# Block-diagonal projection weights and four smaller moves in a fused linear-attention and gated-MLP kernel

## The chip, the cores and the metric

The kernel runs on one core of a Trainium2 chip. The metric is device time in microseconds (us) of one execution; the median of the runs counts. The engines are TensorE (PE; its weight loads are PEld), VectorE (DVE), ScalarE (ACT), GpSimd (POOL) and SyncE (SP), which issues most DMAs.

## The reference

```python
# q, k, v: (8, 8, 576, 64); omega: (128, 64); w_gate, w_val: (512, 1536); w_out: (1536, 512)
scale = 64 ** -0.25
def phi(x):
    proj = np.einsum('bhsd,md->bhsm', x, omega)
    h = proj - np.sum(x * x, axis=-1, keepdims=True) / 2.0
    h = h - np.max(h, axis=-1, keepdims=True)
    return np.exp(h) / np.sqrt(128)
q_p, k_p = phi(q * scale), phi(k * scale)
kv = np.einsum('bhsm,bhsd->bhmd', k_p, v)
z = np.sum(k_p, axis=2)
num = np.einsum('bhsm,bhmd->bhsd', q_p, kv)
den = np.einsum('bhsm,bhm->bhs', q_p, z)[..., None] + 1e-06
x = (num / den).transpose(0, 2, 1, 3).reshape(4608, 512)
g = x @ w_gate
out = (g * (1 / (1 + np.exp(-g))) * (x @ w_val)) @ w_out      # all float32
```

## The kernel before

The attention goes in 72 steps of two groups. A group is 256 rows of two heads of q or of k (or, once per batch element, the 64 rows left over of all eight heads). The first 6 steps have two groups of k, the next 60 one of q and one of k, the last 6 two of q. Stages of several steps are in flight at once:

- `st_transpose(n)`: four TensorE transposes (`pt`) turn the rows of step n, so that the two heads of a group lie one above the other, 64 rows each; ScalarE copies them to `x`, GpSimd squares the rows (`sq`).
- `st_project(n)` (L434): `x` times `omT`, which holds the scaled omega twice, in rows 0 to 63 and in 64 to 127. For each of two groups and two chunks of 128 rows, one matmul per head, on that head's 64 rows. Head 0 writes PSUM bank `pp[0]`, head 1 bank `pp[1]`. An fp32 matmul becomes two instructions, so 8 matmuls stand as 16 in the trace; a transpose stands as one.
- `st_max`, `st_exp`: VectorE's sums and maxima (L448, L455), and eight exponentials on ScalarE into `ph`.
- `k_accumulate(n)`, two steps later: `ph` of k times v, with a column of ones for z, summed in bank `kvacc`; after the last group of a batch element and four heads `kv_finalize` copies it to `kvr`.
- For q of batch elements 0 to 3: `q_transpose` (`ptq`, copied to `qt`), `q_mult` (`po`), a division on VectorE, and `q_out` (`xt`, turned by TensorE, split into `xh` and `xl`).
- For q of elements 4 to 7 the division comes first: `kv_finalize` turns z on TensorE (`zp`) and sends it by DRAM back to all partitions (`zd`, then `zt` in `load_z`); `q_den` multiplies `ph` by z on GpSimd (`jk`) and sums on VectorE; `q_norm` scales `ph` on GpSimd (L548); then `q_transpose` and `q_out` (L653, `kvr` as the stationary operand, one head to each half of the columns).

The MLP follows as rows of x are complete. Three tiles of 512 rows come in visits (L689: gate and value; L698: the output product), the other six in pairs (L928) after the attention. Each fp32 operand is split in a high and a low part and multiplied in three fp32r products. The weights are converted for that by `convert_all` in 36 pieces of 128 x 512, six ticks each, on ScalarE, VectorE and GpSimd, and stored in DRAM (`wscr`).

The order of the work is written out: `CLOSE` lists the stages of a step below `EARLY` (25), `GROUPED` those from there on, with places (`SHARE`) into which the MLP's matmuls are dealt by a course computed in advance. `marks` says how many pieces are to be converted by which step (`want` is `OPS`, 6 ticks, times the mark): from step 6 on, 4.5 by step 25, 9 by step 28. Inside that order each engine's program is laid out by a scheduler, so neighbours can swap.

PSUM has eight banks of 128 x 512 fp32: three for the MLP (`ps_m`, also used by early steps), two for `pp` (`ps_p`), one with tag "b" (`ps_att`), one with tag "t" (`ps_tr`), one for `kvacc` (`ps_k`). `pt` lies in "t". From step 25 on `xt` of a step's first q lies in "t", of a second q in "b"; `ptq` of a first q in "b", of a second in "t".

Of the kernel before, what the change touches and what calls it, by code (L numbers as in the profile page):

```python
# [11 lines left out]
F32 = mybir.dt.float32  # L12
# [11 lines left out]
def kernel(  # L24
# [11 lines left out]
    nc = tc.nc  # L36
# [61 lines left out]
    def ps_att(name, shape):  # L98
        return ps_a.tile(shape, F32, name=name, tag="b")
# [106 lines left out]

    EARLY = whole[1]
    clock = course + 4.0 * np.arange(NN + 1)
    marks = [(6, 0.0), (EARLY, 1.5 * FA), (EARLY + 3, 3 * FA)]
    FIRST_RAW = marks[0][0] - 2  # L210
    for k_ in range(1, NSET):
        at = int(np.searchsorted(course, cum[len(ROUNDS[0]) * k_ - 1]))
# [124 lines left out]

    omT = const.tile([P, M], F32, name="omT")  # L340

    def setup_omega():
        om2 = accp.tile([P, 2, D], F32, name="om2", tag="acc")
        for j in range(2):
            nc.scalar.dma_start(om2[:, j, :], omega)
        pt = ps_moe("pt_om", [P, M])
        nc.tensor.transpose(pt, om2.rearrange("p a d -> p (a d)"), ident)
        nc.scalar.activation(omT, pt, AF.Copy, scale=SCALE)

# [71 lines left out]
    def st_project(n):  # L423
        if n >= NS:
            return
        x, st, sq = sts[n]

        new = ps_moe if n < EARLY and n % 2 else ps_proj
        pp = [new(f"pp{hh}_{n}", [P, 2, CH, M]) for hh in range(2)]
        for i in range(2):  # L430
            for c in range(CH):
                for hh in range(2):
                    r = slice(hh * D, (hh + 1) * D)
                    nc.tensor.matmul(  # L434
                        pp[hh][:, i, c, :], x[r, i, c * P : (c + 1) * P], omT[r], start=True, stop=True
                    )
        sts[n] = st, sq, pp
        return True

# [2 lines left out]
    def st_max(n):  # L442
        if n >= NS:
            return
        st, sq, pp = sts[n]

        with tc.issue_after(biased[0].ins) if biased else ExitStack():
            nc.vector.tensor_reduce(  # L448
                st[:, 0].rearrange("p i c h -> p (i c h)"),
                sq.rearrange("p i c h d -> p (i c h) d"),  # L450
                axis=AX.X,
                op=ALU.add,
            )
        for hh in range(2):
            nc.vector.tensor_reduce(st[:, 1, :, :, hh], pp[hh], axis=AX.X, op=ALU.max, negate=True)  # L455
        s0, s1, s2, s3 = (st[:, j].rearrange("p i c h -> p (i c h)") for j in range(4))
        nc.vector.scalar_tensor_tensor(s2, s0, SQC, s1, op0=ALU.mult, op1=ALU.add)
        biased[:] = [nc.vector.scalar_tensor_tensor(s3, s0, -SQC, s2, op0=ALU.mult, op1=ALU.add)]  # L458
        step_end["v"] = biased[0]
        return True  # L460

    def st_exp(n):
        if n >= NS:
            return
        st, _, pp = sts.pop(n)
        for i, (kind, b, g) in enumerate(steps[n]):
            ph = att.tile([P, CH, 2 * M], F32, name=f"ph{i}_{n}", tag=f"ph{i}", bufs=3)
            for hh in range(2):
                for c in range(CH):
                    step_end["s"] = nc.scalar.activation(  # L470
                        ph[:, c, hh * M : (hh + 1) * M], pp[hh][:, i, c, :],
                        AF.Exp, bias=st[:, 3, i, c, hh : hh + 1], scale=1.0,
                    )
            box[kind, b, g] = ph
        return True
# [7 lines left out]
    def kv_finalize(b, a2):  # L483
        acc = kvacc.pop((b, a2))
        raw = att.tile([P, 4, VW], F32, name=f"kvr{b}_{a2}", tag="kvr", bufs=4)
        nc.scalar.copy(raw, acc)
        for j in range(2):
            kvst[b, 2 * a2 + j] = raw[:, 2 * j : 2 * j + 2, :]
        if b >= BPOOL:

            zp = ps_att(f"zp{b}_{a2}", [4, P])
            nc.tensor.transpose(zp, raw[:, :, D], ident)
            zs = att.tile([4, P], F32, name=f"zs{b}_{a2}", tag="zs")
            nc.scalar.copy(zs, zp)
            zd = dram.tile([4, P], F32, name=f"zd{b}_{a2}", tag="zd", bufs=4)
            nc.sync.dma_start(zd, zs)
            zds[b, a2] = zd

    zds = {}
    zbc = {}  # L500

    def load_z(n):

        for _, b, g, gr in slots(n, "q"):
            if g == 0 and b >= BPOOL:
                zt = att.tile([P, 2, 4, M], F32, name=f"zt{b}", tag="zt")
                for a2 in range(2):
                    nc.sync.dma_start(
                        zt[:, a2], zds.pop((b, a2)).rearrange("(o h) m -> o h m", o=1).broadcast_to([P, 4, M])
                    )  # L510
                    zbc[b, a2] = zt[:, a2]
# [28 lines left out]

    def q_norm(n):
        n -= NLAG
        for _, b, g, gr in slots(n, "q"):
            if b < BPOOL:
                continue
            dn = dns.pop((b, g))
            phv = box["q", b, g].rearrange("p c (h m) -> p (c h) m", m=M)
            nc.gpsimd.tensor_tensor(  # L548
                phv, phv,
                dn[:, 2].rearrange("p c (h o) -> p (c h) o", o=1).broadcast_to([P, 2 * CH, M]),  # L550
                op=ALU.mult,
            )
# [31 lines left out]
    qts = {}  # L584
    xns = {}

    def q_transpose(n):
        m = n
        todo = [(b, g) for _, b, g, gr in slots(n - TLAG, "q") if b < BPOOL]
        todo += [(b, g) for _, b, g, gr in slots(n - NLAG, "q") if b >= BPOOL]  # L590
        for i, (b, g) in enumerate(todo):
            ph = box.pop(("q", b, g))
            pt = (ps_moe if m < EARLY else ps_tr if i else ps_att)(f"ptq{b}_{g}", [P, 2, G])
            for hh in range(2):
                for c in range(CH):
                    nc.tensor.transpose(pt[:, hh, c * P : (c + 1) * P], ph[:, c, hh * M : (hh + 1) * M], ident)  # L596
            qts[b, g] = att.tile([P, 2, G], F32, name=f"qt{b}_{g}", tag="qt", bufs=4)
            nc.scalar.copy(qts[b, g], pt)
# [39 lines left out]
    def q_out(n):  # L638
        n -= OLAG
        for i, b, g, gr in slots(n, "q"):  # L640
            po = (ps_att if n + OLAG < EARLY or i else ps_tr)(f"xt{b}_{g}", [P, G])
            first = column(b, gr)
            if b < BPOOL:
                xn = xns.pop((b, g))
                for c in range(CH):
                    nc.tensor.transpose(po[:, c * P : (c + 1) * P], xn[:, c].rearrange("p h d -> p (h d)"), ident)  # L646
            else:
                qt = qts.pop((b, g))

                segs = [(pr, pr * RES, RES) for pr in range(NPAIR)] if gr is None else [(gr[0], 0, G)]  # L650
                for pr, o, w in segs:
                    for hh in range(2):
                        nc.tensor.matmul(  # L653
                            po[hh * D : (hh + 1) * D, o : o + w], kvst[b, pr][:, hh, 0:D], qt[:, hh, o : o + w],
                            start=True, stop=True, skip_group_check=True,
                        )
            j, o = tile_of(first)
            if gr is None:
                parts_ = [(po.rearrange("d (r c) -> d r c", c=RES), slice(0, NPAIR), j, o, RES)]
            else:  # L660
                cut = min(TILES[j][1] - o, G)
                parts_ = [(po[:, 0:cut], gr[0], j, o, cut)]
                if cut < G:
                    parts_.append((po[:, cut:G], gr[0], j + 1, 0, G - cut))
            for src, pr, j, o, w in parts_:
                if j in x_dram:
                    xo = att.tile(list(src.shape), F32, name=f"xo{b}_{g}_{j}", tag="xo", bufs=3)
                    nc.scalar.copy(xo, src)
                    nc.sync.dma_start(x_dram[j][:, pr, o : o + w], xo)
                    continue  # L670
                if j not in xt:
                    xt[j] = [xres.tile([P, NPAIR, T], F32R, name=f"x{e}{j}", tag=f"x{e}") for e in "hl"]
                hi, lo = (t[:, pr, o : o + w] for t in xt[j])
                nc.scalar.copy(hi, src)
                nc.vector.tensor_tensor(lo, src, hi.bitcast(F32), op=ALU.subtract)
            if gr is None or gr[0] == NPAIR - 1:
                cols_done[0] = first + (RES if gr is None else G)
        return bool(slots(n, "q"))
# [388 lines left out]
    def give(us):  # L1067
# [28 lines left out]
        q_den,  # L1096
    )
    GROUPED = (
        q_out,
        st_project,  # L1100
        q_transpose,
# [84 lines left out]
```

## Time and profile before

| | us |
|---|---|
| runs | 1176.55, 1169.88, 1171.24 |
| median | 1171.24 |
| profiled execution | 1174.65 |
| its span, first to last instruction | 1172.6 |
| TensorE busy | 1145.0 |
| VectorE / ScalarE / GpSimd busy | 703.3 / 684.7 / 588.6 |
| pp, busy time of its 1152 matmuls (L434) | 96.0 |
| normalisation on GpSimd (L548), 36 | 38.2 |

A row of the timeline gives start, length, engine, line, operation, output and inputs, the stationary and moving shapes, the count, and in brackets the idle time of the engine before it and what ended it. A row of the waits gives who waited for whom, us in total, times, and the longest.

### The profile page before, as it was taken

How to read it: one execution, taken by the hardware profiler on the slowest of the kernel's cores; microseconds unless marked ns; L12 is line 12 of the kernel's file. 1: busy time of each engine (PE TensorE's matmuls, PEld its weight loads, DVE VectorE, ACT ScalarE, POOL GpSimd, SP SyncE). 2: the span in 40 equal slices, each digit the busy share in tenths (PEclk: the TensorE clock that was granted, in tenths of full speed). 3: DMA queues.
4: the chain of work that ended last, by engine and by line, in shares of the span. 5: the costliest groups of instructions: out<-in, count | busy, mean ns of one | idle time of the engine just before them, and what ended most of it. 6: DMA issues, size and time to landing. Idle time of an engine off the chain costs nothing.

```text
span 1172.6 us, 18833 instructions
## 1 busy us (share of the span) xinstructions
PE 1145.0 (98%) x6633; PEld 948.3 (81%) x6633; DVE 703.3 (60%) x1266; ACT 684.7 (58%) x1541; POOL 588.6 (50%) x515
## 2 busy tenths in 40 slices
PE   8999999999999999999999999999999999999998
PEld 7888778888787778767778788888878888888886
DVE  3777576454666665556373566666566666456654
ACT  4888887877766866857434544444444445444441
POOL 3332353253656775586335655544455543555551
PEclk9999999999999999999999999999999999999999
DMA  6655355654445543431445111124211111211103
GB/s 141 160 135 132 102 161 142 185 151 122 129 130 139 143 140 102 109 86 55 135 109 151 57 55 55 54 65 124 63 50 46 52 52 46 81 55 54 46 18 72
DMA packets 173965, 114.30 MB, mean 97 GB/s; under 512 B 125840, under 2 KB 144304, under 8 KB 173872
## 3 DMA queue, kind: packets, MB, share of 16 engines
q1 hardware_dynamic: 172528, 112.78, 35.1%
q8 instruction: 52, 0.85, 0.3%
q10 hardware_dynamic: 1344, 0.33, 0.1%
q14 instruction: 41, 0.34, 0.1%
HBM read 87.88 MB, written 25.18 MB: 96 GB/s over the span
## 4 chain that ended last, share of the span: by engine, by line
PE 80%; DVE 7%; ACT 4%; POOL 3%; DMA 3%; issue 2%; SPq 0%; POOLq 0%; DVEq 0%; ACTq 0%
PE o L698 22%; PE a L928 16%; PE c L928 8%; PE g L689 6%; PE pp L434 6%; PE kvacc L572 5%; PE v L689 4%; PE d L928 4%; PE pt L411 3%; PE po L613 3%; PE ptq L596 2%; ACT ph L470 2%; PE xt L653 1%; POOL wlo L252 1%; PE xt L646 1%
## 5 line engine op out<-in xcount | busy, mean ns | idle before, releaser
L470 ACT ACTIVATE ph<-pp,st 128x128 f32<-128x128 f32 x576 | 157.3, 387 | 12.8 <-DVE st L458 12.3
L728 DVE TENSOR_TENSOR acc<-o,acc 128x512 f32<-128x512 f32 x156 | 105.8, 685 | 94.6 <-PE o L698 94.2
L418 POOL TENSOR_TENSOR sq<-nat 128x512 f32<-128x512 f32 x72 | 78.1, 1084 | 156.2 <-DVE st L448 113.5
L915 POOL TENSOR_TENSOR wlo<-wspare,whi 128x512 fp32r<-128x512 f32 (+1 forms) x60 | 60.9, 1036 | 117.4 <-ACT whi L914 111.0
L455 DVE TENSOR_REDUCE st<-pp 128x4 f32<-128x512 f32 x144 | 92.8, 683 | 43.2 <-PE pp L434 42.8
L434 PE MATMUL pp<-omT,x 64*128 64x128 f32 x1152 | 96.0, 296 | 3.4 <-ACT x L419 2.3
L252 POOL TENSOR_TENSOR wlo<-wraw,whi 128x512 fp32r<-128x512 f32 x59 | 82.5, 1404 | 26.9 <-ACT whi L251 23.0
L434 PEld LDWEIGHTS pp<-omT,x 64*128 64x128 f32 x1152 | 78.2, 195 | 20.8 <-issue 10.1
L915 POOL TENSOR_TENSOR wlo<-s,whi 128x512 fp32r<-128x512 f32 x64 | 82.4, 1306 | 3.8 <-ACT whi L914 3.8
L1024 ACT COPY late<-a 128x512 f32<-128x512 f32 x72 | 42.2, 586 | 60.0 <-PE a L928 58.8
L698 PE MATMUL o<-whi,late 128*128 128x512 f32 x192 | 74.5, 389 | 0.0
L572 PE MATMUL kvacc<-v,ph 128*128 128x65 f32 x512 | 69.1, 276 | 0.0
L536 DVE TENSOR_REDUCE dj<-jk 128x4 f32<-128x512 f32 x36 | 24.6, 684 | 73.3 <-POOL jk L532 60.7
L572 PEld LDWEIGHTS kvacc<-v,ph 128*128 128x128 f32 x512 | 66.4, 200 | 0.5
L789 POOL TENSOR_TENSOR hl<-sl,hh 128x512 fp32r<-128x512 f32 x36 | 46.9, 1306 | 34.6 <-ACT hh L788 34.6
L291 POOL TENSOR_TENSOR wc<-st 128x512 int32<-128x512 int32 x36 | 37.4, 1040 | 47.7 <-ACT st L289 25.2
L419 ACT COPY x<-pt 128x512 f32<-128x512 f32 x72 | 43.2, 600 | 28.3 <-PE pt L411 26.9
L689 PE MATMUL g<-xh,whi 128*128 128x512 f32 x144 | 59.5, 414 | 0.0
L1028 DVE TENSOR_TENSOR late<-c,late 128x512 f32<-128x512 f32 x25 | 17.3, 692 | 69.7 <-PE c L928 60.6
L698 PE MATMUL o<-whi,hh 128*128 128x512 f32 x144 | 58.4, 406 | 0.5 <-ACT sl L765 0.4
L689 PE MATMUL v<-xh,whi 128*128 128x512 f32 x144 | 57.7, 401 | 0.0
L689 PE MATMUL g<-xh,wlo 128*128 128x512 f32 x144 | 57.4, 398 | 0.0
(255 smaller groups left out, 3355.7 us busy)
## 6 DMA issues: line engine op xcount, KB each, us to landing
wraw<-wscr SPq DMA_DIRECT2D x63, 256.0 KB, 2.7
wspare<-wscr SPq DMA_DIRECT2D x60, 256.0 KB, 2.7
wscr<-wc SPq DMA_DIRECT2D x36, 256.0 KB, 2.2
out_dram<-acc SPq DMA_DIRECT2D x72, 128.0 KB, 2.4
nat<-in_k_dram SPq DMA_DIRECT2D x64, 128.0 KB, 3.0
nat<-in_q_dram SPq DMA_DIRECT2D x64, 128.0 KB, 3.1
v<-in_v_dram SPq DMA_DIRECT2D x62, 128.0 KB, 3.6
st<-in_moe_w_gate_dram SPq DMA_DIRECT2D x12, 512.0 KB, 3.9
```

Source lines behind the costliest of these rows:

```text
L252: nc.gpsimd.tensor_tensor(lo, raw, hi.bitcast(F32), op=ALU.subtract)
L418: nc.gpsimd.tensor_tensor(sq, nat, nat, op=ALU.mult)
L434: nc.tensor.matmul(pp[hh][:, i, c, :], x[r, i, c * P : (c + 1) * P], omT[r], start=True, stop=True)
L455: nc.vector.tensor_reduce(st[:, 1, :, :, hh], pp[hh], axis=AX.X, op=ALU.max, negate=True)
L470: step_end["s"] = nc.scalar.activation(ph[:, c, hh * M : (hh + 1) * M], pp[hh][:, i, c, :], AF.Exp, bias=st[:, 3, i, c, hh : hh + 1], scal ...
L572: nc.tensor.matmul(acc[:, 2 * (pr % 2) + hh, :], ph[:, c, hh * M : (hh + 1) * M], vt[:, 2 * c + j if gr is None else c, hh, :], start=firs ...
L689: nc.tensor.matmul(ps, a_[:, ws], b_[:, c, :], start=n == 0, stop=n == 3 * NC - 1)
L698: nc.tensor.matmul(ps, a_[:, ts_], b_, start=first and n == 0, stop=last and n == 2)
L728: nc.vector.tensor_tensor(a_, po, a_, op=ALU.add)
L789: nc.gpsimd.tensor_tensor(hl, h, hh.bitcast(F32), op=ALU.subtract)
L915: nc.gpsimd.tensor_tensor(lo, src_, hi.bitcast(F32), op=ALU.subtract)
L928: nc.tensor.matmul(ps, a_[:, w_], b_[:, c, :], start=start and c == 0 and m == 0, stop=c == CH - 1 and m == 2, skip_group_check=True,)
```

## The change

1. `omT` becomes a block diagonal of 128 rows and 2 x 128 columns: omega for head 0 in the upper left, for head 1 in the lower right, zeros elsewhere. A projection is one matmul of 128 rows and 256 columns for each group and chunk, four in a step, and a bank `pp[i]` now holds group i with both heads. The maxima go by group.
2. The conversion of the weights begins with step 5 and has other marks: 6 by step 25, 9 by step 29.
3. `zp`, its copy and its store leave `kv_finalize` for `z_rows`, which stands first in `GROUPED`, so at the head of the next step.
4. `xt` of both q of a step lies in one tile of bank "t". From step 68 on (`KV_END`), `ptq` of a second q lies in the bank of `kvacc`, which nothing else needs by then.
5. In steps with two q, the 12 normalisations of the last six, `q_norm` runs on VectorE. (24 stay on GpSimd.)

```diff
-    marks = [(6, 0.0), (EARLY, 1.5 * FA), (EARLY + 3, 3 * FA)]
+    marks = [(5, 0.0), (EARLY, 2 * FA), (EARLY + 4, 3 * FA)]
...
-    omT = const.tile([P, M], F32, name="omT")
+    omT = const.tile([P, 2, M], F32, name="omT")
...
-        nc.scalar.activation(omT, pt, AF.Copy, scale=SCALE)
+        for j in range(2):
+            r = slice(j * D, (j + 1) * D)
+            nc.vector.memset(omT[r, 1 - j], 0.0)
+            nc.scalar.activation(omT[r, j], pt[r], AF.Copy, scale=SCALE)
...
-        pp = [new(f"pp{hh}_{n}", [P, 2, CH, M]) for hh in range(2)]
+        pp = [new(f"pp{i}_{n}", [P, CH, 2, M]) for i in range(2)]
         for i in range(2):
             for c in range(CH):
-                for hh in range(2):
-                    r = slice(hh * D, (hh + 1) * D)
-                    nc.tensor.matmul(
-                        pp[hh][:, i, c, :], x[r, i, c * P : (c + 1) * P], omT[r], start=True, stop=True
-                    )
+                nc.tensor.matmul(
+                    pp[i][:, c].rearrange("p h m -> p (h m)"),
+                    x[:, i, c * P : (c + 1) * P],
+                    omT.rearrange("p h m -> p (h m)"),
+                    start=True, stop=True,
+                )
...
-        for hh in range(2):
-            nc.vector.tensor_reduce(st[:, 1, :, :, hh], pp[hh], axis=AX.X, op=ALU.max, negate=True)
+        for i in range(2):
+            nc.vector.tensor_reduce(st[:, 1, i], pp[i], axis=AX.X, op=ALU.max, negate=True)
...
-                        ph[:, c, hh * M : (hh + 1) * M], pp[hh][:, i, c, :],
+                        ph[:, c, hh * M : (hh + 1) * M], pp[i][:, c, hh, :],
...
         if b >= BPOOL:
-
+            zraw[b, a2] = raw
...
+    def z_rows():
+
+        for (b, a2), raw in zraw.items():
             zp = ps_att(f"zp{b}_{a2}", [4, P])
...
+                if (b, 1) not in zds:
+                    z_rows()
...
+        by = nc.vector if len(slots(n, "q")) == 2 else nc.gpsimd
...
-            nc.gpsimd.tensor_tensor(
+            by.tensor_tensor(
...
+    KV_END = max(n for n in range(NS) if slots(n, "k")) + KLAG + 1
...
-            pt = (ps_moe if m < EARLY else ps_tr if i else ps_att)(f"ptq{b}_{g}", [P, 2, G])
+            if i and m >= KV_END:
+                pt = ps_k.tile([P, 2, G], F32, name=f"ptq{b}_{g}", tag="kv")
+            else:
+                pt = (ps_moe if m < EARLY else ps_tr if i else ps_att)(f"ptq{b}_{g}", [P, 2, G])
...
-            po = (ps_att if n + OLAG < EARLY or i else ps_tr)(f"xt{b}_{g}", [P, G])
+            if n + OLAG < EARLY:
+                po = ps_att(f"xt{b}_{g}", [P, G])
+            else:
+                if i == 0:
+                    both = ps_tr(f"xt{b}_{g}", [P, 2, G])
+                po = both[:, i]
...
     GROUPED = (
+        lambda n: z_rows(),
         q_out,
```

TensorE's program in an early step, 13, before (a name's last number tells buffers apart; `pp_13_911` and `pp_13_912` are the banks of head 0 and head 1, which go on in turn until each has four):

```order
L572 MATMUL kvacc_1_682<-v_103,ph_10_764 128x65 x2
L434 MATMUL pp_13_911<-omT,x_863 128x128
L613 MATMUL po_4_868<-kvr_0_369,qt_4_824 128x65 x4
L434 MATMUL pp_13_912<-omT,x_863 128x128
...
L646 MATMUL xt_4_926<-ident,xn_4_876 128x128 x2
L411 MATMUL pt_931<-ident,nat_769 128x128 x4
```

And of the changed kernel:

```order
L586 MATMUL kvacc_1_653<-v_104,ph_11_800 128x65
L632 MATMUL po_4_832<-kvr_0_352,qt_4_791 128x65 x4
L435 MATMUL pp_13_875<-omT,x_827 128x256 x2
L435 MATMUL pp_13_876<-omT,x_827 128x256 x2
L414 MATMUL pt_888<-ident,nat_731 128x128 x4
L670 MATMUL xt_4_883<-ident,xn_4_840 128x128 x2
```

The eight matmuls of 64 rows are four of 256 columns, one bank after the other, and here `po` no longer stands between two of them. (A step is split in this way in 16 of the steps 4 to 25 before, in 12 after.)

TensorE's program around step 55, where z of element 5 is turned, before (the `g` rows are the MLP's, `zp` is the turned z):

```order
L689 MATMUL g_7_5034<-xl_641,whi_0_4638 128x512
L492 MATMUL zp_0_4992<-ident,kvr_0_4990 4x128
L572 MATMUL kvacc_1_4998<-vrest_105,ph_52_4790 128x65 x4
...
L653 MATMUL xt_1_5081<-qt_1_4984,kvr_0_4037 64x256 x2
L434 MATMUL pp_55_5090<-omT,x_5029 128x128
L434 MATMUL pp_55_5091<-omT,x_5029 128x128
...
L596 MATMUL ptq_2_5100<-ident,ph_53_4902 128x128 x4
```

And of the changed kernel:

```order
L713 MATMUL g_8_4836<-xh_611,wlo_0_4442 128x512
L503 MATMUL zp_0_4858<-ident,kvr_0_4773 4x128
L677 MATMUL xt_1_4864<-qt_1_4767,kvr_0_3856 64x256 x2
L435 MATMUL pp_55_4873<-omT,x_4806 128x256 x2
L435 MATMUL pp_55_4874<-omT,x_4806 128x256 x2
L615 MATMUL ptq_2_4879<-ident,ph_53_4689 128x128 x4
```

`zp` moved from a place two matmuls into step 54's MLP work to the head of step 55, behind the whole of that work.

GpSimd's program at the first steps with two q to normalise, before (`jk` is q times z, L548 the normalisation, `hl` the MLP's):

```order
L532 TENSOR_TENSOR jk_6_6398<-ph_66_6294,zt_5723 128x512
L532 TENSOR_TENSOR jk_7_6404<-ph_66_6299,zt_5723 128x512
L548 TENSOR_TENSOR ph_66_6294<-ph_66_6294,dj_6_6400 128x512
L548 TENSOR_TENSOR ph_66_6299<-ph_66_6299,dj_7_6406 128x512
L789 TENSOR_TENSOR hl_6_6422<-sl_6_6194,hh_6_6421 128x512
L418 TENSOR_TENSOR sq_6637<-nat_6345 128x512
```

And of the changed kernel:

```order
L545 TENSOR_TENSOR jk_6_6123<-ph_66_6029,zt_5482 128x512
L545 TENSOR_TENSOR jk_7_6129<-ph_66_6034,zt_5482 128x512
L813 TENSOR_TENSOR hl_6_6147<-sl_6_5933,hh_6_6146 128x512
L421 TENSOR_TENSOR sq_6359<-nat_6080 128x512
L541 TENSOR_TENSOR jk_8_6243<-ph_67_6113,zt_5482 64x256 x4
```

The two normalisations left GpSimd; on VectorE each now stands behind the reciprocal that it needs.

More of the change, by code (lines that the diff above doesn't have):

```diff
@@ L489, in kv_finalize @@
         if b >= BPOOL:
+            zraw[b, a2] = raw
+    zraw = {}
+    zds = {}
+    def z_rows():
+        for (b, a2), raw in zraw.items():
             zp = ps_att(f"zp{b}_{a2}", [4, P])
@@ L497, in kv_finalize @@
             zds[b, a2] = zd
-    zds = {}
+        zraw.clear()
     zbc = {}
```

## The prediction

> **What bounds the kernel now.** I read the page's busy times and its chain first, then TensorE's waits, then stretches, then single steps on TensorE.
>
> ```profile
> span 1172.6 us, 18833 instructions
> ...
> PE 1145.0 (98%) x6633; PEld 948.3 (81%) x6633; DVE 703.3 (60%) x1266; ACT 684.7 (58%) x1541; POOL 588.6 (50%) x515
> ...
> PE 80%; DVE 7%; ACT 4%; POOL 3%; DMA 3%; issue 2%; SPq 0%; POOLq 0%; DVEq 0%; ACTq 0%
> ```
>
> TensorE is busy for all but 27.6 us of the span and makes 80% of the chain that ended last. Ends of matmuls are modelled, so that alone would not prove it full; the starts below do. The next question is what it ever waits for. The longest of its waits in the attention (us in total, times, longest):
>
> ```profile
> PE ptq L596 <- ACT xo L668: 3.0, 3, 2.1
> PE pt L411 <- issue: 2.3, 1, 2.3
> PE zp L492 <- ACT kvr L486: 2.1, 3, 1.1
> PE pt L411 <- ACT qt L598: 1.9, 1, 1.9
> PE pt L411 <- DVE xl L675: 1.2, 1, 1.2
> ```
>
> No engine holds TensorE up for more than a few us in all. By stretches (us; the first number of each pair is TensorE's busy time):
>
> ```profile
> core 0: us, PE busy (x) PEld busy (x) DVE busy (x) ACT busy (x) POOL busy (x), PEclk, DMA share, GB/s
> 60.00:95.00 35.00, 34.70 (x340) 31.75 (x340) 27.15 (x75) 30.18 (x91) 12.72 (x12) 1.00 0.55 139
> 130.00:160.00 30.00, 26.41 (x188) 22.06 (x187) 20.79 (x39) 25.08 (x54) 15.31 (x14) 1.00 0.48 141
> 500.00:530.00 30.00, 27.25 (x178) 20.74 (x175) 19.11 (x39) 16.27 (x44) 24.64 (x24) 0.94 0.28 75
> 530.00:560.00 30.00, 27.45 (x180) 21.09 (x179) 17.76 (x37) 21.46 (x55) 21.61 (x21) 1.00 0.22 62
> ```
>
> So a microsecond of TensorE work added in the attention (0 to 570 us) is a microsecond of time nearly everywhere, and what the change can take away is the idle of 130 to 160 and of 500 to 560 us, about 9 us.
>
> **Part 1, omega as a block diagonal.** This decides. A step's projection before is 8 fp32 matmuls, each issued as two instructions of 128 columns on 64 rows; the two heads use different halves of the array's rows. After, it is 4 matmuls, so 8 instructions of 256 columns on all 128 rows, half of them against zeros. A step of before at 164 us
>
> ```profile
> 163.64 0.38 PE L646 MATMUL xt<-ident,xn 128*128 128x128 f32 x2
> 163.95 1.16 PE L434 MATMUL pp<-omT,x 64*128 64x128 f32 x16
> 165.04 0.66 PE L596 MATMUL ptq<-ident,ph 128*128 128x128 f32 x4
> ```
>
> and at 401 us
>
> ```profile
> 400.45 0.65 PE L653 MATMUL xt<-qt,kvr 128*64 128x256 f32 x4
> 401.03 1.16 PE L434 MATMUL pp<-omT,x 64*128 64x128 f32 x16
> 402.12 0.66 PE L596 MATMUL ptq<-ident,ph 128*128 128x128 f32 x4
> ```
>
> and at 65 us
>
> ```profile
> 64.45 1.16 PE L434 MATMUL pp<-omT,x 64*128 64x128 f32 x14
> 65.54 0.44 PE L646 MATMUL xt<-ident,xn 128*128 128x128 f32 x2
> 65.81 0.60 PE L411 MATMUL pt<-ident,nat 128*128 128x128 f32 x4
> 66.25 0.56 PE L572 MATMUL kvacc<-v,ph 128*128 128x65 f32 x4
> ```
>
> with the first two of the next step ahead of po:
>
> ```profile
> 67.58 0.48 PE L434 MATMUL pp<-omT,x 64*128 64x128 f32 x2
> 67.99 1.11 PE L613 MATMUL po<-kvr,qt 128*128 128x65 f32 x8
> ```
>
> From the start of pp to the start of what follows, the 16 take 1.09 us, 68 ns each. One fp32 instruction of 128 columns, alone on the array, has a slot of (66.25 - 65.81) / 4 = 110 ns (the transposes pt). So the 16 run partly side by side, two heads at a time. The full-width form has no such partner. Its price comes from two rows:
>
> ```profile
> L653 PE MATMUL xt<-qt,kvr x192: 219/379/690, 309.4 to 570.7; 128*64 128x256 f32 x128, 128*64 128x64 f32 x64
> L434 PE MATMUL pp<-omT,x x1152: 272/272/580, 6.4 to 546.4; 64*128 64x128 f32 x192
> ```
>
> The median xt has 256 columns and lasts 379 ns, the pp with 128 lasts 272: 128 columns more cost 107 ns, so 256 columns stream in 214 ns. Bounds of a slot: below, 110 ns (the transpose's, were columns free); above, 228 ns (the 214 plus a margin of 14, an estimate). I take 214, the row of the same size, so 8 x 0.214 = 1.71 us per step.
>
> Middle: 2 transposes ahead need 0.22 of the 0.31 us before pp, so entering the 64-row form costs 0.09; before is 1.18, the change +0.53. Late: xt ahead uses half the columns, and its switch stays, so +0.62. Early: pp is mostly split around po (1.09 + 0.41 + two switches of 0.09 = 1.68), so +0.03 for a split step and +0.53 for a whole one. How many steps (16 instructions each):
>
> ```profile
> core 0: us, PE busy (x) PEld busy (x), PEclk, DMA share, GB/s
> 0.00:26.00 26.00, 8.32 (x64) 7.14 (x64) 1.00 0.65 149
> 26.00:130.00 104.00, 31.86 (x352) 24.60 (x352) 1.00 0.53 129
> 130.00:316.00 186.00, 24.33 (x320) 20.31 (x320) 1.00 0.53 148
> 316.00:560.00 244.00, 31.49 (x416) 26.13 (x416) 0.99 0.41 113
> ```
>
> Early 22 steps: in the order of before, 16 are split and 6 whole: 0.5 + 3.2 = +3.7. Middle 20 x 0.53 = +10.6. Late 26 x 0.62 = +16.1. Some five steps of before already run up to 0.5 us longer than 1.09: -2. Sum **+28 us**, none of it covered, since TensorE's queue goes straight on with the next work.
>
> The first four steps are slower by a factor of about two:
>
> ```profile
> 10.23 2.08 PE L434 MATMUL pp<-omT,x 64*128 64x128 f32 x16 [0.67 <-ACT x L419]
> 12.25 1.11 PE L411 MATMUL pt<-ident,nat 128*128 128x128 f32 x4
> 13.15 3.08 PE L572 MATMUL kvacc<-v,ph 128*128 128x65 f32 x14
> ```
>
> The four pt take 0.90 us there against 0.44 later, although the PEclk column says 1.00. At that pace 8 x 0.428 = 3.42 against 2.02: +1.4 each, +5.6 if all four stay slow. [...] Between -4 and +5.6 I take +2, a little to the side of the slow slots that the trace does show.
>
> [...]
>
> Two half-height copies of omT and two memsets at the start replace one copy: 0 to +0.3. Maxima and exponentials keep number and size; the first maximum can begin after half of the matmuls.
>
> **Part 2, z at the next step's head.** The same 8 transposes, 8 copies and DMAs. The three waits of zp on kvr (2.1 us) go, since a whole step's head lies between: -2 (0 to -2.1). Its DMAs and the broadcast issue later on SP's queue, but two steps ahead of the first q_den that reads them.
>
> **Part 3, both turned x in one bank; the second turned q in the kv bank.** Only for steps with two q, the last ones. The turned q no longer waits for xo (3.0 us), and pt no longer for qt (1.9). Now pt waits for both xo instead; the turned q stands ahead of it as cover.
>
> **Part 4, twelve normalisations from GpSimd to VectorE.** Two of them in a row, and a VectorE operation of the same size:
>
> ```profile
> 520.10 2.04 POOL L548 TENSOR_TENSOR ph<-ph,dj 128x512 f32<-128x512 f32 x2
> 520.29 0.68 DVE L785 TENSOR_TENSOR sl<-v,sl 128x512 f32<-128x512 f32 x1
> ```
>
> GpSimd gives up 12 x 1.02 = 12 us of its 46 in 500 to 560; VectorE takes 12 x 0.68 = 8 on its 37 of 60, where each now stands ahead of the next pair's small operations; a turned q waits for it as it did for GpSimd's. Parts 3 and 4 serve the same waits: 3.0 + 1.9, and 0.06 x 30 = 1.8 us for the 0.94 in the clock column: -5 (0 to -6.7).
>
> **Part 5, conversion begins at step five, 6 pieces instead of 4.5 by step 25, 9 by step 29 instead of 28.** The work is the same. The waits of pt at 136 and 159 us (1.2 + 2.3) stand behind xl, and xl behind conversion on VectorE. Fewer pieces there, and pp between xt and pt lasts 0.5 us longer: -2 (0 to -3.5). Its price is 1.5 pieces more in 26 to 130 us for ScalarE, which has three operations of this size in a piece:
>
> ```profile
> L289 ACT ACTIVATE st<-st x36: 648/726/768, 42.9 to 496.2; 128x512 int32<-128x512 uint32 x36
> ```
>
> That is 1.5 x 3 x 0.73 = 3.3 us on an engine busy 30.18 of 35: hidden as long as TensorE is the fuller one, +3 if not.
>
> **The sum.** +28 +2 -2 -5 -2 = +21, and 1 more of the 3 for ScalarE's early pieces: +22. The profiled execution took 1174.65 us (span 1172.6), 3.4 above the median 1171.24; so 1196.7 in that execution, **1193** in the median's terms.
>
> **Rivals.** [...] *Nothing given back*: the slow start costs +5.6, ScalarE becomes the bound of the early steps (+3), and of the 9 only 3 come: +34, 1205. *Faster*: the full-height instruction does not pay by column. At the transposes' 110 ns a step has 0.88 us, 0.83 less than the forecast's, 72 times: 22 - 60 = -38, 1133. It turns from slower to faster at (28 + 2 - 9 + 1) / 72 = 0.31 less per step, 1.40 us, 175 ns an instruction; the xt row says 214. *No change that can be told*: 165 to 185 ns an instruction.
>
> **Chances.** Forecast 0.58, full clock early 0.17, nothing given back 0.17, no change 0.04, faster 0.04; the last two are small because they need a slot that no row of 256 columns shows. The range 1181 to 1207 takes in the first three with 2 us beyond the ends; a measurement of this kernel tells 0.5% (5.9 us) from no change. All three are slower by more: slower 0.92, same 0.04, faster 0.04.
>
> **What would show it.** Right: pp appears 576 times with 128x256, its busy time goes from 96.0 to about 120 us, 1.71 us from its start to the next kind; TensorE's waits at zp, at ptq for xo and at pt near 522 us are gone, GpSimd's L548 group has 24. Wrong: pp's slot is under 180 ns; or the first 26 us shrink; or new waits stand before pp (on x) or ptq (on the normalisations now queued on VectorE). From 610 us on nothing should differ but the shift.

## Result: 2.5% slower, and the profile after

The changed kernel takes 1201.42 us (median of 4 runs, 1200.76 to 1204.94) against 1173.34 for the kernel before (4 runs): ratio 1.0246, 95% interval 1.0206 to 1.0286, so +28 us. The forecast was 1193 in 1181 to 1207, +22 on the median of 1171.24 that it started from. Ratios compare fast runs alone; the one slow run, of the block diagonal with x ahead, took 1958.85 us at a granted clock of 0.557 and counts only in that kernel's median.

The page after: totals, the group of pp, and the chain that ended last.

```profile
span 1199.6 us, 17638 instructions
...
PE 1174.6 (98%) x6057; PEld 975.0 (81%) x6057; DVE 718.3 (60%) x1280; ACT 685.6 (57%) x1540; POOL 579.6 (48%) x503
...
PE 85%; DVE 8%; issue 2%; DMA 2%; POOL 2%; ACT 2%; SPq 0%; POOLq 0%; DVEq 0%; ACTq 0%
...
L435 PE MATMUL pp<-omT,x 128*128 128x256 f32 x576 | 147.2, 395 | 1.8 <-ACT x L422 1.7
```

The span grew by 27.0 us, TensorE's busy time by 29.6, with 1195 instructions fewer in all and 576 fewer on TensorE. One step's projection in the middle of the attention and a late one:

```profile
163.25 0.38 PE L670 MATMUL xt<-ident,xn 128*128 128x128 f32 x2
163.47 1.89 PE L435 MATMUL pp<-omT,x 128*128 128x256 f32 x8
165.20 0.60 PE L615 MATMUL ptq<-ident,ph 128*128 128x128 f32 x4
```

```profile
430.70 0.65 PE L677 MATMUL xt<-qt,kvr 128*64 128x256 f32 x4
431.28 1.99 PE L435 MATMUL pp<-omT,x 128*128 128x256 f32 x8
433.11 0.60 PE L615 MATMUL ptq<-ident,ph 128*128 128x128 f32 x4
```

From pp's start to the next kind it is 165.20 - 163.47 = 1.73 us in the middle and 1.83 late, where it was 1.09: 216 ns an instruction in the middle. The entry from the transposes has no gap any more (0.22 for two). Then TensorE's waits:

```profile
PE xt L677 <- ACT x L422: 7.7, 4, 3.6
PE pt_om L347 <- DMA om<-in_omega_dram: 3.9, 1, 3.9
PE ptq L615 <- ACT zs L505: 2.4, 1, 2.4
PE pp L435 <- ACT x L422: 1.7, 3, 0.7
```

The waits named in the forecast are gone (zp for kvr, ptq for xo, pt for qt, pt for xl), and two stand there that before does not show: xt for ScalarE's copy of x, and ptq for the copy of the turned z. The longest wait, on ScalarE and on TensorE:

```profile
446.83 0.38 ACT L490 COPY kvr<-kvacc 128x260 f32<-128x260 f32 x1
448.59 2.18 ACT L474 ACTIVATE ph<-pp,st 128x128 f32<-128x128 f32 x8 [1.38 <-DVE st L462]
450.60 0.64 ACT L422 COPY x<-pt 128x512 f32<-128x512 f32 x1
```

```profile
447.41 0.27 PE L503 MATMUL zp<-ident,kvr 128*4 128x128 f32 x1
451.29 1.12 PE L677 MATMUL xt<-qt,kvr 128*64 128x256 f32 x4 [3.61 <-ACT x L422]
452.34 3.78 PE L435 MATMUL pp<-omT,x 128*128 128x256 f32 x8
```

xt is to be written to the bank "t", where pt still waits to be copied to x; the copy stands on ScalarE behind eight exponentials, which wait for VectorE. The projection behind it takes 3.6 us instead of 1.83. The stretches say why; the column PEclk is the granted clock:

```profile
core 0: us, PE busy (x) PEld busy (x) DVE busy (x) ACT busy (x) POOL busy (x), PEclk, DMA share, GB/s
440.00:447.00 7.00, 7.00 (x42) 5.56 (x41) 3.07 (x5) 2.63 (x6) 5.39 (x5) 1.00 0.55 185
447.00:451.00 4.00, 0.68 (x4) 0.23 (x2) 3.05 (x5) 2.62 (x10) 2.97 (x4) 0.94 0.31 72
451.00:457.00 6.00, 5.71 (x18) 4.14 (x19) 2.53 (x6) 3.08 (x6) 3.25 (x3) 0.50 0.10 34
```

The stall of 3.6 us is followed by 6 us at a granted clock of 0.50. So the starts of pp, step by step (after less before, from the two timelines), show slopes, some jumps, and a start that came earlier:

| steps | difference at the first and at the last, us | what it is |
|---|---|---|
| 0 to 4 | +0.6, -4.2 | full clock from 10.2 us on instead of 25.2 |
| 4 to 25 | -4.2, +1.3 | projection, +0.26 a step |
| 25 to 31 | +1.3, -0.3 | conversion's stalls gone |
| 31 to 58 | -0.3, +12.9 | projection, +0.5 a step, stalls at xt included |
| 58 to 60 | +12.9, +18.8 | the stall and the half clock above |
| 60 to 71 | +18.8, +26.7 | projection, +0.7 a step, stalls included |

### The profile page after: what moved, and what is told of

It reads as the page before. It is cut to its first block, busy times and chain, and to the rows that moved or that the text cites. A ratio compares the mean times of both kernels' runs of the same rounds, so it can differ in the third digit from the quotient of the medians.

```text
span 1199.6 us, 17638 instructions
## 1 busy us (share of the span) xinstructions
PE 1174.6 (98%) x6057; PEld 975.0 (81%) x6057; DVE 718.3 (60%) x1280; ACT 685.6 (57%) x1540; POOL 579.6 (48%) x503
## 4 chain that ended last, share of the span: by engine, by line
PE 85%; DVE 8%; issue 2%; DMA 2%; POOL 2%; ACT 2%; SPq 0%; POOLq 0%; DVEq 0%; ACTq 0%
PE o L722 22%; PE a L952 15%; PE pp L435 10%; PE c L952 8%; PE g L713 7%; PE v L713 5%; PE kvacc L586 5%; PE d L952 4%; PE po L632 2%; PE pt L414 2%; PE ptq L615 2%; PE xt L677 1%; DMA first_b<-xs 1%; DVE st L459 1%; PE xt L670 1%
## 5 line engine op out<-in xcount | busy, mean ns | idle before, releaser
L435 PE MATMUL pp<-omT,x 128*128 128x256 f32 x576 | 147.2, 395 | 1.8 <-ACT x L422 1.7
L459 DVE TENSOR_REDUCE st<-pp 128x4 f32<-128x512 f32 x144 | 97.8, 687 | 52.2 <-PE pp L435 51.3
L435 PEld LDWEIGHTS pp<-omT,x 128*128 128x128 f32 x576 | 104.8, 194 | 24.8 <-issue 5.4
L617 ACT COPY qt<-ptq 128x512 f32<-128x512 f32 x72 | 42.0, 588 | 45.9 <-PE ptq L615 45.2
L586 PE MATMUL kvacc<-v,ph 128*128 128x65 f32 x512 | 66.2, 269 | 0.0
L586 PEld LDWEIGHTS kvacc<-v,ph 128*128 128x128 f32 x512 | 63.7, 193 | 0.5 <-ACT kvr L490 0.3
L713 PE MATMUL g<-xl,whi 128*128 128x512 f32 x144 | 56.9, 395 | 0.0
```

The source lines that it names most:

```text
L435: nc.tensor.matmul(pp[i][:, c].rearrange("p h m -> p (h m)"), x[:, i, c * P : (c + 1) * P], omT.rearrange("p h m -> p (h m)"), start=True, ...
L459: nc.vector.tensor_reduce(st[:, 1, i], pp[i], axis=AX.X, op=ALU.max, negate=True)
L586: nc.tensor.matmul(acc[:, 2 * (pr % 2) + hh, :], ph[:, c, hh * M : (hh + 1) * M], vt[:, 2 * c + j if gr is None else c, hh, :], start=firs ...
L713: nc.tensor.matmul(ps, a_[:, ws], b_[:, c, :], start=n == 0, stop=n == 3 * NC - 1)
```

## Experiments

Each ratio is to the kernel before on the same chip (medians there 1172.7 to 1174.9 us).

**The block diagonal alone, and all the rest alone.** Edits: hunks 2 to 6 of the diff (omT, st_project, the maxima and the exponentials' input) put into the kernel before; then all other hunks without these.

> The kernel before with the block-diagonal omega alone, nothing else of the change. Theory A (the loss is the lost overlap of the two heads on TensorE, all of it): pp 576 times with a slot of 1.73 to 1.83 us per step against 1.09 to 1.18, +34 us over 68 steps, full clock already at about 10 us (-4): +30 us, and the other parts together are worth about -2. Theory B (the other parts carry a good part of the loss, by new waits on the bank of z and on x): this kernel is only 20 to 24 us slower than before, and the stall of TensorE with half clock at 447 to 457 us is not in it.

> The change without its first part: omega and projection as before, all other parts as in the change. Theory A: the small waits go and little comes, -2 to -8 us, 1165 to 1171. Theory B: the moved z and the shared bank bring waits of their own, +4 to +8 us; xt waits for x, and ptq for the copy of z, as in the change.

The block diagonal alone: 1203.53 us, ratio 1.0262 (1.0235 to 1.0289), +30. The rest alone: 1173.69, ratio 1.0007 (0.9993 to 1.0020). So the first part carries the whole loss, as theory A had it, and the rest gives nothing in sum, which is neither A's gain nor B's loss. A is not the whole story either. Waits of xt for x (4.7 us) and half-clock windows (granted clock 0.994 over the run) are in the kernel with the block diagonal alone. So they do not come from the other parts, as B had it, and A's sum by slots does not hold them.

**Full height without the 256 columns.** Is it the lost overlap or the form? omT gets its zeros as in the change, the banks stay by head:

```diff
-    r = slice(hh * D, (hh + 1) * D)
-    nc.tensor.matmul(pp[hh][:, i, c, :], x[r, i, c * P : (c + 1) * P], omT[r], start=True, stop=True)
+    nc.tensor.matmul(pp[hh][:, i, c, :], x[:, i, c * P : (c + 1) * P], omT[:, hh], start=True, stop=True)
```

> The kernel before with 16 projection instructions of 128 columns in a step as before and the same banks, but each on all 128 rows, against omega with the other head's rows zero. Theory A (full height, so no two heads side by side): 16 x 0.108 = 1.73 us a step, the same time as the block diagonal alone within 2 us, +28 to +32. Rival (the cost is in the form of 256 columns or in banks by group): as before within 4 us, a step's projection 1.1 us.

1194.39 us, ratio 1.0181 (1.0156 to 1.0205): +21. A projection of the middle in this kernel:

```profile
167.02 1.95 PE L436 MATMUL pp<-omT,x 128*128 128x128 f32 x16
168.80 0.60 PE L598 MATMUL ptq<-ident,ph 128*128 128x128 f32 x4
```

It takes 1.78 us, 111 ns an instruction, where the same 16 on half the rows took 1.09: the overlap is lost without the 256 columns. In its size neither expectation holds: full height costs 21 us with 16 instructions of 128 columns, and the block diagonal costs 9 more. The granted clock is 1.000 over the whole run here, where the block diagonal's is 0.994. The starts of pp in the two agree within about 1 us from step 29 to step 51 (+12.0 for the block diagonal, +13.0 here); then they part, to +29.6 and +20.6 at step 71. In ScalarE's program the copy of x stands behind all eight exponentials in 9 of the steps 26 to 71 before and here, in 42 with the block diagonal alone and in 40 with the whole change. That gave a new theory, C: the copy of x is late, and the stalls and half clock come from it.

**The banks alone.** The same 16 instructions, but with the change's banks by group:

```diff
-        pp = [new(f"pp{hh}_{n}", [P, 2, CH, M]) for hh in range(2)]
+        pp = [new(f"pp{i}_{n}", [P, CH, 2, M]) for i in range(2)]
...
-                        pp[hh][:, i, c, :], x[:, i, c * P : (c + 1) * P], omT[:, hh], start=True, stop=True
+                        pp[i][:, c, hh, :], x[:, i, c * P : (c + 1) * P], omT[:, hh], start=True, stop=True
```

(and the maxima and the exponentials by group, as in the change).

> As the kernel with 16 projection instructions on all 128 rows, but the banks by group as in the change, not by head. That alone makes ScalarE's program put the copy of x behind the eight exponentials in most steps from 26 on, where the one with banks by head has it ahead. Theory C (the late copy of x holds TensorE up at xt, which needs the same bank, and the idle stretches bring half clock): 1201 to 1206, 7 to 11 us above the 1194 of the kernel with banks by head, with several waits of xt for ACT x and half-clock windows. Rival (the form of 256 columns or chance placed those stalls): 1194 within 3 us.

1205.56 us, ratio 1.0265 (1.0243 to 1.0287): 10 us more than with banks by head by the ratios, 11 by the medians, as theory C has it. ScalarE at the same step, first with banks by head, then by group:

```profile
400.11 0.59 ACT L422 COPY x<-pt 128x512 f32<-128x512 f32 x1 [0.76 <-PE pt L414]
400.97 2.17 ACT L472 ACTIVATE ph<-pp,st 128x128 f32<-128x128 f32 x8 [0.28 <-DVE st L460]
```

```profile
402.18 2.18 ACT L472 ACTIVATE ph<-pp,st 128x128 f32<-128x128 f32 x8 [1.72 <-DVE st L460]
404.20 0.64 ACT L422 COPY x<-pt 128x512 f32<-128x512 f32 x1
```

ScalarE sits idle for 1.72 us with the copy of x behind what it waits for, and TensorE waits at xt (by group):

```profile
404.89 0.65 PE L655 MATMUL xt<-qt,kvr 128*64 128x256 f32 x4 [1.83 <-ACT x L422]
```

That the order flips with the banks alone is seen in the programs. Why the scheduler swaps the two is argued, not shown: with one bank complete after half of the projection, the first maximum and the first exponentials come due earlier in its plan.

**The copy of x put ahead, and behind.**

```diff
     GROUPED = (
...
+        lambda n: st_transpose(n + 1),
         st_max,
         st_exp,
         q_den,
-        lambda n: st_transpose(n + 1),
```

> The block diagonal alone, and the transposes of the next step moved ahead of the maxima in the written order, so that the copy of x stands before or among the first two exponentials. Theory C: the waits of xt for x go, and the time comes down from 1203 to 1192 to 1196. Rival: 1203 within 3 us.

The block diagonal with x ahead: 1194.19 us, ratio 1.0164 (1.0136 to 1.0192), +19 and no more. The wait of xt for x shrinks from 4.7 us (3 times) to 0.2 (once). That is theory C from the other side, with two limits. The copy is late in 42 steps, but up to step 51 that costs nothing: pp of step 51 starts within 0.2 us of this kernel's, and the 10 us fall behind. And the longest wait is not one for x. In the block diagonal alone, from step 58 to 59, 3.9 of the 10 us are lost where the turned z waits for the copy of kvr, with half clock behind it:

```profile
452.60 0.27 PE L496 MATMUL zp<-ident,kvr 128*4 128x128 f32 x1 [2.42 <-ACT kvr L490]
```

This wait is as long (2.43 us) in the other two kernels with x behind (banks by group, and before with x behind), and 0.16 to 1.14 us in this kernel, in full height with banks by head and in before. So it goes with the place of x, but the chain from one to the other is not shown.

```diff
-        nc.scalar.copy(x, pt)
+        with tc.issue_after(step_end["s"].ins) if n > EARLY + 1 else ExitStack():
+            nc.scalar.copy(x, pt)
```

> The kernel before with the copy of x forced behind the exponentials in all steps from 27 on, its projection untouched. Theory C: xt waits for x in many steps; the projection that leads up to it is shorter here, so the waits are as long or longer: +7 to +14 us. Rival (without the longer projection there is slack for it): within 3 us of before.

The kernel before with x behind: 1179.83 us, ratio 1.0045 (1.0027 to 1.0063), +5. In its trace pp of step 51 starts 6.2 us earlier than in the profiled before, most of that from the clock's earlier rise, and that of step 59 starts 2.8 later: 9 us lost in eight steps, with 10.2 us at half clock from 369 us on. The sign is C's, the medians' size is below its range. In the trace the late copy costs the short projection 9.5 us from step 51 to 71, close to the 10 to 12 that it costs the long one over the same steps (the block diagonal without and with x ahead, full height with banks by group and by head). Why the medians show half of that is open: the profiled run began 4.8 us ahead by its clock, and the other executions were not profiled.

**The start.** The block diagonal in step 0 alone (in the other steps the two halves as before, from a second tile). In the changed kernel's trace the projection of step 0 runs from 7.00 us to the next work at 10.41, and the full clock begins at 10.24; pp of step 4 starts there at 22.25 us.

> The kernel before with the block diagonal in step 0 alone. Theory (one projection that fills the array for 3 us brings the full clock): step 4 begins its projection at about 22 us instead of 26.5 and the kernel is 3 to 5 us faster, 1168 to 1170. Rival (the clock comes from the dense array over several steps): full clock no earlier than 20 us, time as before or 1 us longer.

1172.70 us, ratio 1.0007 (0.9981 to 1.0032): no gain. In the trace the full clock comes at 10 us and step 4 starts at 22.0 instead of 26.5, but a half-clock window at 27 takes most of it back (PEclk reads 1.00 also ahead of the first entry in a trace's clock record, in before from 10 to 16 us with the first entry at 25.2; the times of the rise are from that record, and in this trace the pace changes with it):

```profile
0.00:27.00 27.00, 19.32 (x159) 16.38 (x161) 12.30 (x28) 16.36 (x51) 9.03 (x26) 1.00 0.67 156
27.00:30.50 3.50, 3.50 (x24) 3.28 (x22) 2.13 (x5) 1.13 (x4) 1.04 (x1) 0.51 0.56 127
```

And the kernel with all but the block diagonal, whose first projections are those of before, had the full clock at 10 us as well:

```profile
10.21 1.16 PE L434 MATMUL pp<-omT,x 64*128 64x128 f32 x16 [0.68 <-ACT x L419]
11.31 0.66 PE L411 MATMUL pt<-ident,nat 128*128 128x128 f32 x4
11.80 1.45 PE L582 MATMUL kvacc<-v,ph 128*128 128x65 f32 x12
```

Before has 2.08 us for that same projection. Over the traces with the old projection the full clock begins at 9.5, 9.6, 10.5, 13.5, 19.0, 25.1, 25.2 and 25.5 us. With a full-height projection in step 0 it begins at 10.0, 10.2, 10.3, 15.4, 15.7 and 16.3 us. So the early rise came without the dense array too, and the -4 us of the profiled run need not be the change's. That the dense array never came as late as four of the other eight may be chance: one trace of each kernel does not tell.

**The other parts.** The conversion's marks alone; z alone; the banks of xt and ptq with the normalisations on VectorE.

> The kernel before with the new marks of the conversion alone. Theory of the prediction: the stalls of 1.2 and 2.3 us at pt near 136 and 159 us go, -2 us (0 to -3.5). Rival: the earlier pieces cost the early steps as much: 0 within 1 us, with the early steps later by 1 to 2 us at step 25.

> The kernel before with z turned at the next step's head, nothing else. Theory of the prediction: the waits of zp for kvr (2.0 us in all) go, -2 us. Theory D (the turned z holds the bank of the turned q until ScalarE has copied it, and the copy stands behind the exponentials): ptq waits for the copy zs, pp waits for ph after step 51, +2 to +5 us.

> The kernel before with both turned x in one bank, the second turned q in the kv bank, and the twelve normalisations on VectorE. Theory of the prediction: the waits of ptq for xo and of pt for qt go and with them the half-clock window at 522 us, -5 us (0 to -6.7). Rival: pt and xt now wait for one another's bank and VectorE for more of its own, 0 within 2 us.

The conversion: 1169.33 us, ratio 0.9956 (0.9936 to 0.9976), -5; in the trace steps 23 to 26 start 0.7 to 1.0 us later than before, step 27 starts 2.9 us earlier, and from step 31 on every step keeps 2.9 to 3.0. TensorE's waits from 120 to 170 us, before and with the new marks:

```profile
PE pt L411 <- issue: 2.3, 1, 2.3
PE pt L411 <- DVE xl L675: 1.2, 1, 1.2
```

```profile
PE pt L411 <- issue: 0.3, 1, 0.3
```

z: 1175.60 us, ratio 1.0015 (0.9999 to 1.0032): no gain, rather a loss. The waits of zp for kvr are gone, 2.1 us, and these two have come or grown (pp for ph was 1.0 in the kernel before):

```profile
PE pp L434 <- ACT ph L470: 3.6, 3, 1.9
...
PE ptq L605 <- ACT zs L501: 2.0, 2, 1.5
```

The turned z now sits in bank "b" ahead of the turned q, which waits until ScalarE comes to the copy, as theory D has it. pp's longest wait is another thing: at 373 us six of the eight exponentials stand behind a cast of weights that waits for its DMA.

The banks and normalisations: 1175.73 us, ratio 1.0013 (0.9996 to 1.0030). TensorE's waits from 500 to 570 us, with them:

```profile
PE xt L664 <- ACT x L419: 1.5, 1, 1.5
PE pp L434 <- ACT ph L470: 1.2, 1, 1.2
PE zp L492 <- ACT kvr L486: 1.0, 1, 1.0
```

The 4.9 us for xo and qt are gone and 2.7 us for x and ph have come. That they come because VectorE does two normalisations ahead of the maxima is argued from its program. At 524 us a half-clock window of 6.8 us stands in place of one of 3.4.

**Together, without what costs.** The conversion with x ahead, and both with the banks and normalisations.

> The conversion's new marks, and the transposes of the next step ahead of the maxima. Theory C with the conversion's -3: in the 8 to 11 steps where before had the copy of x behind the exponentials it is ahead now; -3 to -5 us, 1168 to 1171. Rival: the copy of x ahead delays the exponentials instead, no better than the conversion alone or worse by up to 3 us.

> The conversion's marks, the banks, the normalisations on VectorE and the transposes ahead of the maxima; z and omega as before. If theory D is right on z and the prediction on the banks: -6 to -9 us, the fastest here, 1164 to 1168. Rival: as e11, the banks and VectorE give nothing.

1168.53 us, ratio 0.9961 (0.9944 to 0.9977), and 1171.68, ratio 0.9978 (0.9963 to 0.9993). Both beat before by less than 0.5%, and neither beats the conversion alone beyond its interval. x ahead gives before nothing that shows (it is behind in only 9 steps there), and the banks and normalisations give nothing on top: the forecast of 1164 to 1168 for the second kernel missed.

## Why the prediction was right, and where only in the sum

Its direction and range held, and so did its first mechanism: the lost overlap of the two heads on the array makes up two thirds of the loss. But +22 and +28 agree partly by luck, because errors of both signs cancelled.

| term | forecast | measured | by |
|---|---|---|---|
| longer projection | +28 | +19 to +21 | full height with banks by head; block diagonal with x ahead |
| copy of x behind the exponentials | none | +9 to +11 | the same two kernels with x behind |
| clock at the start | +2 | 0 (-2 to +4) | block diagonal in step 0 alone |
| z | -2 | +2 (0 to +4) | alone |
| banks and normalisations | -5 | +2 (0 to +4) | alone |
| conversion, with the +1 on ScalarE | -1 | -5 (-3 to -8) | alone; -2.9 in its trace |

- *The slot.* 214 ns was forecast from the xt row; 216 in the middle is measured, and 229 (1.83 / 8) behind xt in half the columns. The step that failed is the next one, "none of it covered", which made +28 of what measures +19 to +21. From step 31 to 44 a step grew by 9.72 - 9.35 = 0.37 us, not 0.53; from 46 to 51 by 9.20 - 8.63 = 0.57, not 0.62. Two things took up part of it. The forecast priced the switch into the 64-row form (0.09 us) and not the one out of it: the four turned q behind pp lasted 0.66 us and last 0.60 now, which is 4 us in 68 steps. And TensorE has less idle. The rows are from pp of step 4 to pp of step 71, the second number is TensorE's busy time: before, at full height with banks by head, and with the block diagonal and x ahead.

```profile
26.50:545.50 519.00, 505.67 (x3753) 421.92 (x3752) 326.08 (x727) 394.32 (x1003) 267.94 (x237) 1.00 0.49 131
24.60:566.10 541.50, 535.76 (x3753) 470.90 (x3752) 324.97 (x728) 396.08 (x1002) 268.52 (x237) 1.00 0.46 125
24.20:564.70 540.50, 532.56 (x3221) 449.03 (x3219) 337.12 (x728) 395.12 (x1002) 268.56 (x237) 1.00 0.46 126
```

Idle is 13.3, 5.7 and 7.9 us. So 5 to 8 us of the longer projection went into idle, some of it idle that the forecast had kept for parts 2 to 5 to remove. From step 4 to 25 these two kernels lose more than the 3.7 us of the forecast, 4.9 and 6.4.

- *The copy of x.* The forecast named new waits of pp on x as a thing that would prove it wrong; they came at xt instead. It had read only TensorE's and GpSimd's order. ScalarE's order of copies and exponentials was there to be compared, with the copy last in 40 steps where it had been last in 9.
- *z and the banks.* The waits to be removed were removed. Each time the wait that came next was not priced: the turned z holds a bank until ScalarE copies it, and VectorE's maxima stand behind its new normalisations, which take 0.88 us each in the changed kernel where the forecast had 0.68. The rival "nothing given back" was right in this, and wrong in its slow start and in its 3 us of ScalarE's early pieces: with the conversion's marks alone the early steps are at most 2.0 us later than before, 1.0 at step 26, and the gain of 2.9 us comes behind.
- *The conversion.* Right in its mechanism, the stall of pt behind xl. In the trace its size is within the forecast's 0 to 3.5 us; the medians' -5 (-3 to -8) is beyond it or at its upper end.
- *The clock at the start.* The +2 was chosen between -4 and +5.6. No run shows the -4, or the early full clock that has 0.17 among the chances, as an effect of a fuller array. The full clock did come early in the profiled run, at 10.2 us, but in some traces with the old projection it came as early (9.5 to 10.5 us). In three others it came at 25.1 to 25.5 us, in before at 25.2 although TensorE was busy for all of the 10 us from 16 to 26. With the block diagonal in step 0 alone the time changed by 0 (-2 to +4).
- *The signs.* pp stands 576 times with 256 columns and GpSimd's normalisations 24 times, as forecast. The busy time of pp is 147.2 us and not 120: it counts each projection with its modelled end, 1.89 to 1.99 us in the rows above, and not the 1.73 to 1.83 to the next start. Of the signs against the forecast one came, shorter first steps: pp of step 4 starts 4.2 us earlier, by the clock.

## What to carry to other kernels

Two half-height matmuls on different rows of the array ran side by side here, 68 ns each against 111 when each had the full height; merging them with zeros halved the instructions (1152 to 576) and lengthened a step's projection (1.09 to 1.73 us and more). When a change alters which bank is complete first, compare the program of every engine that reads the banks, not only that of the engine changed: a copy that moved behind its neighbours came with a loss half as large as that of the matmuls, 9 to 11 us beside 19 to 21. A wait taken away is worth its length only less the wait that comes next, so price the holder of the bank after the move.

## What the runs showed of the chip that was not expected

- A short idle of TensorE cost more than its length. Behind idle of 3.6 us up to 451 us the granted clock is 0.50 over the 6 us from 451 us on, and the projection there takes 3.6 us for 1.83; behind 1.88 us idle up to 400 us in the same run it stays at 1.00.
- Idle of nearly the same length had half clock behind it in one place and full clock in another. In the clock records of before and of the changed kernel, every stretch of half clock up to the last change is 3.41 us long or twice that, and every stretch of full clock a whole multiple of 3.413 us: 498.35 and 645.12 us in before (146 and 189 times), 440.32, 88.75 and 648.53 us in the changed kernel (129, 26 and 190 times). So the time of these traces can be parted into stretches of 3.41 us at whose ends the clock changed. With the block diagonal alone, idle of 1.90 us up to 404 us lies in one stretch, and the next is at half clock:

```profile
402.03:405.44 3.41, 1.51 (x9) 0.94 (x9) 1.24 (x3) 3.39 (x12) 2.65 (x2) 1.00 0.90 207
405.44:408.85 3.41, 3.41 (x14) 2.86 (x12) 2.28 (x7) 2.16 (x3) 2.57 (x3) 0.50 0.31 79
```

  In the changed kernel the 1.88 us up to 400 us are parted between two stretches, with 0.95 and 0.93 us, and the clock stays full:

```profile
395.96:399.37 3.41, 2.46 (x11) 1.69 (x9) 3.08 (x5) 1.78 (x8) 2.38 (x3) 1.00 0.83 249
399.37:402.79 3.42, 2.49 (x13) 1.85 (x14) 1.47 (x4) 3.40 (x8) 2.11 (x3) 1.00 0.89 229
402.79:406.20 3.41, 3.39 (x28) 3.06 (x27) 3.34 (x5) 3.22 (x7) 3.00 (x3) 1.00 0.20 30
```

  In the traces of before and of the changed kernel, half clock followed the three stretches at full clock that held 1.89, 2.41 and 2.88 us of idle, and none of the other 675, which held up to 1.61 (idle as the matmuls' starts and modelled ends give it).
- The first full clock came between 9.5 and 25.5 us in programs with the same first steps. At the start of step 4 the early ones (up to 19.0 us) are 3 to 5.5 us ahead of before, about what two of these parts were meant to bring.
- A change between fp32 instructions on half of the array's rows and on all of them cost TensorE time at both ends: 0.09 us on entry (two transposes took 0.31 us to the start of pp, 0.22 when pp had full height) and 0.06 on leaving (four turned q lasted 0.66 us behind pp, 0.60 when it had full height). Behind instructions on half of the columns a late projection took 0.10 us longer than one behind transposes (1.83 for 1.73).
